# Inverse transform: left-over rows through DRAM scratch from tile 3 on, in four parts, with another scratch layout and two writes on ScalarE's queue

## The chip, the cores and the metric

The kernel runs on one core of a Trainium2 chip. The metric is the time of one execution in device microseconds (us). TensorE, VectorE, ScalarE and GpSimd compute; SyncE issues most of the DMAs, and ScalarE and GpSimd can issue some from their own queues.

## What is computed

An FNet-like block and a gated one, both with a residual, in float32. The weights of the first are a filter in the frequency domain:

```python
def _A_ref(x, w_r, w_i):
    B, S, D = x.shape                                  # 1, 2048, 640
    X = jnp.fft.rfft2(x, axes=(-2, -1))
    X = X * (w_r + 1j * w_i)
    return jnp.fft.irfft2(X, s=(S, D), axes=(-2, -1))

def _B_ref(x, w_gate, w_up, w_down):                   # 640 -> 1728 -> 640
    return ((x @ w_gate) * (x @ w_up)) @ w_down

h = x + _A_ref(_layernorm(x), w_r, w_i)
h2 = h + _B_ref(_layernorm(h), w_gate, w_up, w_down)
```

## The kernel before

The 2048 positions are 16 tiles of 128 rows (`NT`). The kernel has stages that follow each other on TensorE: the transform along 640 and 2048 forwards, the filter, the transform along 2048 backwards, the transform along 640 backwards (the inverse stage here), and the gated block in two halves of eight tiles.

The inverse stage takes tile after tile. For tile `t`, `id_mm(t)` (L731) multiplies four blocks of 128 frequencies from `qm` with the table `imt` (128x161 each); the trace shows two instructions for each. Of 642 frequency rows 130 are left over: 64 rows and one edge row for the real and for the imaginary part. They lie in `qr`, split in a high and a low half so that the fast type loses nothing, high in partitions 0 to 63, low in 64 to 127. There are two ways to multiply them:

- plain: five products of 128x322 straight from `qr`;
- stacked: four products of 162 columns with 99 rows each, for which high rows, low rows and high rows again stand below one another (`SI[t]`, three times 33). To be brought into that order the rows make a round trip: `ispread` writes them from `qr` to a DRAM scratch `ifar` (four DMAs and one for the edge rows), and `istack` reads them back (one DMA for 66 rows, one for 33).

Before the change tiles 0 to 4 are plain, tiles 5 to 15 are stacked. The scratch has two parts: tiles 5 to 8, and 9 to 15. `IPARTS` names three reads: tiles 5 to 8 and, once they are done, 12 to 15 go to a stretch of the tile `xt` (named `near` in the code, `xt` in the trace), tiles 9 to 11 go to the tile tagged `dC` (`si` in the trace).

After `id_mm`, `unfold` (L743) copies one half of the sum with ScalarE (`s`, L750), adds and subtracts on VectorE (`q`), folds out on VectorE or GpSimd (`yt`), and `is1_mm` multiplies the 128-point transform (`y<-yt,tab` in the trace). The order on TensorE is tile 0, 1, 2, 3, then `y` of tile 0, tile 4, `y` of tile 1, tile 5 and so on; `id_mm` runs three tiles ahead of `y`.

The last rows of `qr` are written on VectorE just before the stage: high rows at L562, low rows at L563, and row 0 of both halves for the edge at L559 and L560.

The order of the program is written out by hand (`manual_schedule`); each engine runs its own instructions in that order. SyncE's queue holds around the stage: the load of `raw` (`wlast`), part one of the scratch and its read, part two, two loads of `raw` (`wgu`, weights of the gated block), the read of tiles 9 to 11. The read of tiles 12 to 15 follows when tile 8's products have been issued (L742). Each DMA takes the next of eight landing semaphores and first waits that the DMA which used it before has landed.

Of the kernel before, what the change touches and what calls it, by code (L numbers as in the profile page):

```python
# [11 lines left out]
F32 = mybir.dt.float32  # L12
F32R = mybir.dt.float32r
# [3 lines left out]
P = 128  # L17
S, D, NF, FF = 2048, 640, 321, 1728
NT = S // P
# [6 lines left out]
RWHERE = ((1, 0), (0, 0), (1, 160), (0, 160))  # L26
RW = (160, 194, 162, 162)
PLAIN, MID = 5, 10
IPLAIN, IFAR = 5, 9
SUMS = 7  # L30
IPARTS = ((5, 4), (9, 3), (12, 4))
AGAIN = {0: (5, 3, "dC"), 1: (8, 2, "qt"), 4: (10, 3, 0), 7: (13, 3, 1)}
NR = 4
AHEAD = 5
# [15 lines left out]
def f32(ap):  # L50
    return ap.bitcast(F32)
# [29 lines left out]
def tile_spectral_glu(ctx: ExitStack, tc: tile.TileContext, x, wre, wim, wgu, wlast, wdown, wdlast,  # L81
                      cc, ci, fmain, frem, imain, irem, mm, out):
    nc = tc.nc
# [4 lines left out]
    far = ctx.enter_context(tc.tile_pool(name="far", bufs=1, space=bass.MemoryType.DRAM))  # L88
# [210 lines left out]
    def rest_high(a, b):  # L299
        act(s1r[:, 0, a:b], rest[:, a:b], AF.Copy)  # L300
# [114 lines left out]
    def load_mm(g, way):  # L415
        if g < NG:
            nc.sync.dma_start(mms[g % 4][:, way], mm[g][:, way])
# [165 lines left out]
    for g in range(NG - 1):  # L583
        s2_mm(g)
        load_mm(g + 4, 0)
        if g + 2 < NG:
            d_mm(g + 2)
        if g + 3 == NG:
            xt = home("big", [P, 2, 5, 2, 512], "xt", F32R)
            flat = xt[:, 1].rearrange("p k l n -> p (k l n)")  # L590
            irt, sirt = cut(flat, 0, 5, NQ), cut(flat, 5 * NQ, 4, 162)
            scrap, near = cut(flat, 2258, D), cut(flat, 2258 + D, 4, 4, P)
        if g == NG - 2:
            nc.gpsimd.dma_start(flat[:, 0:2258], irem)
        if g == NG - 2:
            s2_mm(g + 1)
            filt_half(g, 0, True, (lambda: is2_out(g - 2),))
        if g >= 1:
            is2_mm(g - 1)
            load_mm(g + 3, 1)  # L600
        if g < NG - 2:
            add = filt(g)
        else:
            direct, _ = filt_half(g, 1)
            direct()
            late = [filt_half(g + 1, 0), filt_half(g + 1, 1, True)]
            high, end, low, main, edges = is2_parts(g - 1)
            late[0][0]()
            high(copy)
            end(copy)  # L610
            low()
            late[0][1]()
            late[1][1]()
            main(slice(0, 4))
            edges(nc.gpsimd)
        if g + 3 < NG:
            load_w(g + 3)
        if g >= 4 and g in AGAIN:
            stack(*AGAIN[g])
        if g == 0:  # L620
            rest_high(MID, NG)
        elif g == 1:
            rest_low(MID, NG)
            qr = home("qr", [P, 2, NT, P], "qr", F32R)
        if g + 2 < NG:
            d_out(g + 2, (0,))
            if 1 <= g < NG - 3:
                high, end, low, main, edges = is2_parts(g - 1)
                high(copy)
                end(copy)  # L630
            d_out(g + 2, (1,))
            add()
            if 1 <= g < NG - 3:
                low()
                main(slice(0, 4))
                edges(nc.gpsimd)
        if g < 2:
            stack(*AGAIN[g])
        elif g == 2:
            spread(MID, NG)  # L640
        if g == 9:
            nc.sync.dma_start(cit, ci)
            nc.sync.dma_start(imt, imain)
# [62 lines left out]
    PE_, PY, YT, Z = {}, {}, {}, {}  # L706

    SI = {}
    ifar = [(a, far.tile([2, 2, 2, 33, b - a, P], F32, name="ifar")) for a, b in ((IPLAIN, IFAR), (IFAR, NT))]

    def ispread(a, o):
        ts = slice(a, a + o.shape[4])
        for h in (1, 0):
            for l in range(2):
                r = 64 * l + 31 * h
                nc.sync.dma_start(o[:, h, l, 1 - h:33].rearrange("b r t n -> r b t n"),
                                  f32(qr[r:r + 32 + h, :, ts]))
        e = f32(qr[0:65:64, 1, ts])
        nc.sync.dma_start(o[:, 0, :, 0].rearrange("b l t n -> l b (t n)"),
                          bass.AP(tensor=e.tensor, offset=e.offset,  # L720
                                  ap=[list(e.ap[0]), [0, 2], [1, P * o.shape[4]]]))

    def istack(t, n):
        o = near[:, :, 0:n] if t != 9 else home("dC", [P, 4, 3, P], "si", F32R)
        a, i = ifar[t >= IFAR]
        src = i[:, :, :, :, t - a:t - a + n].rearrange("b h l r t n -> (l r) (b h) (t n)")
        nc.sync.dma_start(f32(o[0:66]).rearrange("p q t n -> p q (t n)"), src)
        nc.sync.dma_start(f32(o[66:99]).rearrange("p q t n -> p q (t n)"), src[0:33])
        for i in range(n):
            SI[t + i] = o[:, :, i]  # L730

    def id_mm(t):
        ps = PE_[t] = pair("eo")
        main = [(b, o, 161, qm[:, c, t], imt[:, c]) for c, (b, o) in enumerate(((0, 0), (1, 0), (0, 161), (1, 161)))]
        if t not in SI:
            parts((ps[:, 0], ps[:, 1]), main,
                  [(b, qr[:, k, t], irt[:, c]) for c, b, k in ((0, 0, 0), (2, 0, 0), (1, 1, 1), (3, 0, 1), (4, 1, 1))])
            return
        parts((ps[:, 0], ps[:, 1]), main, [])
        for q, (b, h) in enumerate(((0, 0), (0, 1), (1, 0), (1, 1))):  # L740
            mmx(ps[:, b, 160 * h:160 * h + 162], SI[t][0:99, q], sirt[0:99, q], False, h == 1)
        if t == 8:  # L742
            istack(*IPARTS[2])  # L743

    def unfold(t, side, turns=(), extra=()):
        ps = PE_[t]
# [149 lines left out]
    for ts in (range(3), range(3, 6), range(6, 8)):  # L896
        n, t0 = len(ts), ts[-1] + 1
# [11 lines left out]
    tside[NT - 1] = []  # L909
    raw0 = home("dA", [P, 3, D], "raw0")  # L910
    jobs = load_direct(0, [raw0[:, i] for i in range(3)], mid=(
        lambda: ispread(*ifar[0]), lambda: istack(*IPARTS[0]), lambda: ispread(*ifar[1])))
    istack(*IPARTS[1])
    for i, (h, l) in enumerate((h, l) for hs, ls in jobs for h, l in zip(hs, ls)):
        aside[2 + i] += [h, l]
    id_mm(0)
# [287 lines left out]
    for n, (blk, p) in enumerate(steps):  # L1204
# [133 lines left out]
        else:  # L1338
            fs = down_products(*prev, (0, 1)) + down_products(*prev, (2, 3))
            flat = iter(sum(fs, []))  # L1340
# [221 lines left out]
```

## Time and profile before

| what | us |
|---|---|
| median of 3 runs (671.66 to 671.91) | 671.69 |
| the profiled execution | 671.72 |
| its span | 669.9 |
| TensorE busy in the span | 661.1 |
| VectorE, GpSimd, ScalarE busy | 469.1, 394.1, 321.6 |
| products of the inverse stage, first to last start | 106.8 to 148.3 |

Times inside the span count from its start. PE is TensorE's multiplication, PEld its weight load, which runs ahead of it; DVE is VectorE, ACT ScalarE, POOL GpSimd, SP SyncE, and SPq SyncE's queue of DMA issues. A name such as `eo<-xt,si` is the written tile and the read ones, and L121 is the line of the helper that issues nearly all products. The granted TensorE clock is 1.0 throughout. A row of an issue tells how long the queue was occupied by it, not how long the transfer took.

### The profile page before, as it was taken

Reading aid. Unit: us, or ns where it says so; the run is one execution under the profiler, and the core shown is the slowest. Engines: PE = TensorE matmul, PEld = TensorE weight load, DVE = VectorE, ACT = ScalarE, POOL = GpSimd, SP = SyncE. Lnnn points to the kernel's source line nnn. Section 1 sums busy time; section 2 is a strip of 40 time slices with the busy share of each in tenths; the row PEclk is TensorE's granted clock in tenths of the full one; section 3 lists DMA queues with packets and bytes.
Section 4 is the critical chain, followed back from the end, with each engine's and each line's share of the span. In section 5 each row is a group of like instructions: output and inputs, shape, how many; then the busy total and the mean of one; then the engine's idle time right before and its main releaser. Section 6 shows DMA issues by size and latency. Waiting matters only on the chain.

```text
span 669.9 us, 10244 instructions
## 1 busy us (share of the span) xinstructions
PE 661.1 (99%) x3695; PEld 588.4 (88%) x3695; DVE 469.1 (70%) x953; ACT 321.6 (48%) x621; POOL 394.1 (59%) x377
## 2 busy tenths in 40 slices
PE   7999999999999999999999999999999999999997
PEld 7999999887888888888888899888888888888887
DVE  6969997788767767594857567754757475757644
ACT  6977773585525244453626146534434251624220
POOL 3101124750397977968696445198786869697610
PEclk9999999999999999999999999999999999999999
DMA  8638874502212120142332467212011121212004
GB/s 316 230 111 279 245 250 144 172 2 79 79 40 80 39 79 21 33 105 60 98 79 83 95 132 261 79 40 73 14 37 75 41 78 40 79 40 80 1 0 158
DMA packets 48953, 66.12 MB, mean 99 GB/s; under 512 B 24082, under 2 KB 30670, under 8 KB 48774
## 3 DMA queue, kind: packets, MB, share of 16 engines
q1 hardware_dynamic: 48246, 62.91, 30.4%
q0 software_dynamic: 288, 2.16, 0.8%
q8 instruction: 29, 0.48, 0.3%
q10 hardware_dynamic: 368, 0.39, 0.2%
q14 instruction: 22, 0.18, 0.1%
HBM read 54.61 MB, written 10.84 MB: 98 GB/s over the span
## 4 chain that ended last, share of the span: by engine, by line
PE 95%; ACT 2%; DVE 2%; DMA 1%; issue 0%; DVEq 0%
PE e L121 50%; PE d L121 26%; PE eo L121 4%; PE y L121 2%; PE re L121 2%; PE u L476 2%; PE im L121 2%; PE im L527 2%; PE im L270 2%; PE ir L527 1%; DMA x<-in_x_dram 1%; ACT s L296 1%; ACT fold L212 0%; ACT fold L211 0%; PE y L803 0%
## 5 line engine op out<-in xcount | busy, mean ns | idle before, releaser
L121 PE MATMUL e<-xt,wst 128*128 128x512 f32 x864 | 211.1, 390 | 0.0
L121 PEld LDWEIGHTS e<-xt,wst 128*128 128x128 f32 x864 | 160.6, 188 | 31.7
L1082 DVE TENSOR_TENSOR x<-d,x 128x320 f32<-128x320 f32 x280 | 120.3, 482 | 41.2 <-PE d L121 37.0
L121 PE MATMUL d<-wd,ht 128*128 128x320 f32 x832 | 142.1, 309 | 0.0
L121 PEld LDWEIGHTS d<-wd,ht 128*128 128x128 f32 x832 | 129.6, 188 | 5.2
L996 POOL TENSOR_TENSOR wst<-raw,wst 128x1024 fp32r<-128x1024 f32 x23 | 55.5, 2412 | 69.4 <-ACT wst L995 69.4
L121 PE MATMUL e<-t,wst 128*128 128x512 f32 x360 | 94.0, 391 | 0.0
L121 PEld LDWEIGHTS e<-t,wst 128*128 128x128 f32 x360 | 66.7, 188 | 13.0
L121 PE MATMUL d<-wt,ht 128*128 128x320 f32 x360 | 68.9, 309 | 0.0
L1012 POOL TENSOR_TENSOR wst<-raw,wst 128x896 fp32r<-128x896 f32 (+1 forms) x46 | 65.3, 1445 | 0.2 <-ACT wst L1007 0.2
L121 PEld LDWEIGHTS d<-wt,ht 128*128 128x128 f32 x360 | 57.3, 188 | 0.8
L1098 ACT ACTIVATE ht<-e 128x512 fp32r<-128x512 f32 x44 | 26.4, 600 | 49.3 <-DVE e L1160 23.7
L1007 ACT ACTIVATE wst<-raw 128x896 fp32r<-128x896 f32 (+1 forms) x48 | 30.1, 676 | 31.2 <-POOL raw L1001 30.4
L1156 DVE TENSOR_TENSOR e<-e,h 128x512 f32<-128x512 f32 x24 | 16.8, 699 | 39.4 <-ACT wst L1007 23.2
L1057 DVE TENSOR_TENSOR x<-d,x 128x320 f32<-128x320 f32 x62 | 27.5, 485 | 22.5 <-PE d L121 22.4
L688 ACT ACTIVATE wd<-draw 128x320 fp32r<-128x320 f32 (+1 forms) x30 | 15.7, 561 | 55.2 <-POOL draw L698 52.4
L121 PE MATMUL e<-xt,wdir 128*128 128x512 f32 x180 | 41.9, 392 | 0.0
L1136 ACT ACTIVATE h<-e 128x512 f32<-128x512 f32 x24 | 14.3, 596 | 56.8 <-PE e L121 56.8
L121 PEld LDWEIGHTS e<-xt,wdir 128*128 128x128 f32 x180 | 33.4, 188 | 7.5 <-ACT xt L813 0.5
L1101 DVE TENSOR_TENSOR ht<-e,ht 128x512 fp32r<-128x512 f32 x54 | 36.9, 685 | 1.6 <-ACT ht L1098 1.3
L1153 ACT ACTIVATE h<-e 128x512 f32<-128x512 f32 x24 | 14.3, 597 | 46.6 <-PE e L121 46.6
L667 POOL TENSOR_TENSOR wd<-draw,wd 128x640 fp32r<-128x640 f32 x8 | 12.5, 1582 | 40.8 <-ACT wd L666 40.8
(241 smaller groups left out, 1190.6 us busy)
## 6 DMA issues: line engine op xcount, KB each, us to landing
raw<-in_wgu_dram SPq DMA_DIRECT2D x24, 640.0 KB
draw<-in_wdown_dram SPq DMA_DIRECT2D x24, 320.0 KB
wts<-in_wre_dram SPq DMA_DIRECT2D x16, 322.0 KB
x<-in_x_dram SPq DMA_DIRECT2D x15, 320.5 KB
out_dram<-x SPq DMA_DIRECT2D x15, 320.0 KB
bits<-in_mm_dram SPq DMA_DIRECT2D x32, 128.0 KB
wts<-in_wim_dram SPq DMA_DIRECT2D x9, 322.0 KB
zfar<-zr SPq DMA_DIRECT2D x32, 80.0 KB
```

The costliest lines, as they stand in the source:

```text
L121: nc.tensor.matmul(o, l, r, start=start, stop=stop, skip_group_check=True)
L527: nc.tensor.matmul(out, y[:, h, a:b], inv(g, h), start=n == 0, stop=n == len(ys) - 1)
L688: act(o[:, 0, a:a + n], src, AF.Copy)
L996: ptt(wa[:, 1], stage[:, 0:1024], f32(wa[:, 0]), op=OP.subtract)
L1007: act(ws[:, 0, o:o + b - a], stage[:, a:b], AF.Copy)
L1012: ptt(ws[:, 1, o:o + b - a], stage[:, a:b], f32(ws[:, 0, o:o + b - a]), op=OP.subtract)
L1057: tt(xv, ps[b][:, 0:320], xv, op=OP.add)
L1082: tt(xv, o, xv, op=OP.add)
L1098: act(hop[:, a, 0], src, AF.Copy)
L1101: engine.tensor_tensor(hop[:, a, 1], src, f32(hop[:, a, 0]), op=OP.subtract)
L1136: act(h0, oa, AF.Copy)
L1156: tt(ob, ob, h1, op=OP.add)
```

## The change

- Tiles 3 and 4 become stacked. `IPARTS` now lists four parts, tiles 3 and 4, 5 to 8, 9 to 11, 12 to 15, each with its tile: parts 0 and 2 the one tagged `dC`, parts 1 and 3 the stretch of `xt`.
- Each part has a scratch of its own. Its dims were (part of the spectrum, half, copy, row, tile, column), and are now (copy, row, part, half, tile, column), so that what one partition reads, four pieces of 512 bytes times the number of tiles, is one contiguous run. The stretch of `xt` is cut anew for each part, so that the run is contiguous there as well.
- The order is: write part 0, write part 1, read part 0, read part 1, the two `raw` loads, write part 2, read part 2, write part 3; the read of part 3 stays at tile 8.
- For part 0 the two writes with `h` = 1 go out on ScalarE's queue; all others stay on SyncE's.

```diff
-IPLAIN, IFAR = 5, 9
-IPARTS = ((5, 4), (9, 3), (12, 4))
+IPARTS = ((3, 2, "dC"), (5, 4, "near"), (9, 3, "dC"), (12, 4, "near"))
...
-            scrap, near = cut(flat, 2258, D), cut(flat, 2258 + D, 4, 4, P)
+            scrap, near = cut(flat, 2258, D), cut(flat, 2258 + D, 16 * P)
...
-    ifar = [(a, far.tile([2, 2, 2, 33, b - a, P], F32, name="ifar")) for a, b in ((IPLAIN, IFAR), (IFAR, NT))]
+    ifar = [far.tile([2, 33, 2, 2, n, P], F32, name="ifar") for _, n, _ in IPARTS]
-    def ispread(a, o):
-        ts = slice(a, a + o.shape[4])
+    def ispread(i, queue=nc.sync):
+        t, n, _ = IPARTS[i]
         for h in (1, 0):
             for l in range(2):
                 r = 64 * l + 31 * h
-                nc.sync.dma_start(o[:, h, l, 1 - h:33].rearrange("b r t n -> r b t n"),
-                                  f32(qr[r:r + 32 + h, :, ts]))
+                (queue if h else nc.sync).dma_start(ifar[i][l, 1 - h:33, :, h].rearrange("r b t n -> r b (t n)"),
+                                                    f32(qr[r:r + 32 + h, :, t:t + n]).rearrange("r b t n -> r b (t n)"))
...
-    def istack(t, n):
-        o = near[:, :, 0:n] if t != 9 else home("dC", [P, 4, 3, P], "si", F32R)
-        a, i = ifar[t >= IFAR]
-        src = i[:, :, :, :, t - a:t - a + n].rearrange("b h l r t n -> (l r) (b h) (t n)")
-        nc.sync.dma_start(f32(o[0:66]).rearrange("p q t n -> p q (t n)"), src)
-        nc.sync.dma_start(f32(o[66:99]).rearrange("p q t n -> p q (t n)"), src[0:33])
+    def istack(i):
+        t, n, tag = IPARTS[i]
+        if tag == "near":
+            o = cut(near, 0, 4, n, P)
+        else:
+            o = home(tag, [P, 4, n, P], "si", F32R)
+        src = ifar[i].rearrange("l r b h t n -> (l r) (b h t n)")
+        nc.sync.dma_start(f32(o[0:66]).rearrange("p q t n -> p (q t n)"), src)
+        nc.sync.dma_start(f32(o[66:99]).rearrange("p q t n -> p (q t n)"), src[0:33])
...
     jobs = load_direct(0, [raw0[:, i] for i in range(3)], mid=(
-        lambda: ispread(*ifar[0]), lambda: istack(*IPARTS[0]), lambda: ispread(*ifar[1])))
-    istack(*IPARTS[1])
+        lambda: ispread(0, nc.scalar), lambda: ispread(1), lambda: istack(0), lambda: istack(1)))
+    ispread(2)
+    istack(2)
+    ispread(3)
```

SyncE's queue from the load of `wlast` on, before the change (written and read tile, then partitions and elements):

```order
L665 DMA raw_1299<-in_wlast_dram 128x640
L716 DMA ifar<-qr 33x2x512 x2
L716 DMA ifar<-qr 32x2x512 x2
L719 DMA ifar<-qr 2x2x512
L727 DMA xt<-ifar 66x4x512
L728 DMA xt<-ifar 33x4x512
L716 DMA ifar<-qr 33x2x896 x2
L716 DMA ifar<-qr 32x2x896 x2
L719 DMA ifar<-qr 2x2x896
L665 DMA raw_1299<-in_wgu_dram 128x640 x2
L727 DMA si<-ifar 66x4x384
L728 DMA si<-ifar 33x4x384
```

The same place after it; L715 is the line of the writes, L718 of the edge rows, L728 and L729 of the reads:

```order
L664 DMA raw_1301<-in_wlast_dram 128x640
L715 DMA ifar<-qr 64x1x256 x2
L718 DMA ifar<-qr 2x2x256
L715 DMA ifar<-qr 66x1x512 x2
L715 DMA ifar<-qr 64x1x512 x2
L718 DMA ifar<-qr 2x2x512
L728 DMA si<-ifar 66x1024
L729 DMA si<-ifar 33x1024
L728 DMA xt<-ifar 66x2048
L729 DMA xt<-ifar 33x2048
L664 DMA raw_1301<-in_wgu_dram 128x640 x2
```

Eight writes stand ahead of the first read where five stood, and the first read is now that of tiles 3 and 4. The two writes missing from part 0 stand on ScalarE, between the last copy into `qm` and `s` of tile 0.

TensorE from tile 3's main products to those of tile 5, before:

```order
L121 MATMUL eo<-tab,qm 128x161 x4
L121 MATMUL eo<-xt,qr 128x322 x5
L121 MATMUL y<-yt,tab 128x320 x2
L121 MATMUL eo<-tab,qm 128x161 x4
L121 MATMUL eo<-xt,qr 128x322 x5
L121 MATMUL y<-yt,tab 128x320 x2
L121 MATMUL eo<-tab,qm 128x161 x4
```

And after:

```order
L120 MATMUL eo<-tab,qm 128x161 x4
L120 MATMUL eo<-xt,si 128x162 x4
L120 MATMUL y<-yt,tab 128x320 x2
L120 MATMUL eo<-tab,qm 128x161 x4
L120 MATMUL eo<-xt,si 128x162 x4
L120 MATMUL y<-yt,tab 128x320 x2
L120 MATMUL eo<-tab,qm 128x161 x4
```

Only the left-over products of tiles 3 and 4 differ, and they now read `si`, which comes by DMA. On VectorE and GpSimd no instruction moves.

More of the change, by code (lines that the diff above doesn't have):

```diff
@@ L715, in ispread @@
                 r = 64 * l + 31 * h
-                nc.sync.dma_start(o[:, h, l, 1 - h:33].rearrange("b r t n -> r b t n"),
-                                  f32(qr[r:r + 32 + h, :, ts]))
[L718 to L721, printed above, removed]
-    def istack(t, n):
-        o = near[:, :, 0:n] if t != 9 else home("dC", [P, 4, 3, P], "si", F32R)
-        a, i = ifar[t >= IFAR]
-        src = i[:, :, :, :, t - a:t - a + n].rearrange("b h l r t n -> (l r) (b h) (t n)")
[L727 to L730, printed above, removed]
+                (queue if h else nc.sync).dma_start(ifar[i][l, 1 - h:33, :, h].rearrange("r b t n -> r b (t n)"),
+                                                    f32(qr[r:r + 32 + h, :, t:t + n]).rearrange("r b t n -> r b (t n)"))
+        e = f32(qr[0:65:64, 1, t:t + n])
+        nc.sync.dma_start(ifar[i][:, 0, :, 0].rearrange("l b t n -> l b (t n)"),
+                          bass.AP(tensor=e.tensor, offset=e.offset, ap=[list(e.ap[0]), [0, 2], [1, P * n]]))
+    def istack(i):
[7 more added lines that the diff above has]
+        nc.sync.dma_start(f32(o[66:99]).rearrange("p q t n -> p (q t n)"), src[0:33])
+        for j in range(n):
+            SI[t + j] = o[:, :, j]
     def id_mm(t):
@@ L742, in id_mm @@
         if t == 8:
-            istack(*IPARTS[2])
+            istack(3)
     def unfold(t, side, turns=(), extra=()):
```

## The prediction

> **What bounds the kernel now.** I read the page first, then TensorE's waits, then the inverse stage engine by engine in order of time. The page says that TensorE is busy for nearly the whole span:
>
> ```profile
> span 669.9 us, 10244 instructions
> PE 661.1 (99%) x3695; PEld 588.4 (88%) x3695; DVE 469.1 (70%) x953; ACT 321.6 (48%) x621; POOL 394.1 (59%) x377
> ```
>
> TensorE's waits between 107 and 157 us, which is the inverse stage and what follows it, are one line (total, times, longest):
>
> ```profile
> PE eo L121 <- ACT qm L556: 0.3, 1, 0.3
> ```
>
> So what TensorE saves here shortens the span, and what it waits here lengthens it. TensorE in order of time (start, duration, line, output<-inputs), tiles 3, 4 and 5:
>
> ```profile
> 112.65 1.26 PE L121 MATMUL eo<-tab,qm 128*128 128x161 f32 x8
> 113.64 1.00 PE L121 MATMUL eo<-xt,qr 128*128 128x322 f32 x5
> 114.48 1.24 PE L121 MATMUL y<-yt,tab 128*128 128x320 f32 x4
> 115.56 1.26 PE L121 MATMUL eo<-tab,qm 128*128 128x161 f32 x8
> 116.55 1.01 PE L121 MATMUL eo<-xt,qr 128*128 128x322 f32 x5
> 117.40 1.24 PE L121 MATMUL y<-yt,tab 128*128 128x320 f32 x4
> 118.47 1.26 PE L121 MATMUL eo<-tab,qm 128*128 128x161 f32 x8
> 119.46 0.68 PE L121 MATMUL eo<-xt 99*128 99x162 f32 x4
> 119.98 1.28 PE L121 MATMUL y<-yt,tab 128*128 128x320 f32 x4
> ```
>
> A plain tile reads its left-over rows straight from `qr` (five products); a stacked one, tile 5, reads them from a tile that came through DRAM (four narrower products, input `xt`). The stacked tile is shorter, but its input must have landed. SyncE's queue for that round trip, each row one or more DMA issues:
>
> ```profile
> 107.04 2.19 SPq L716 DMA_DIRECT2D ifar<-qr  x4
> 109.28 0.57 SPq L719 DMA_DIRECT2D ifar<-qr  x1
> 111.28 0.29 SPq L727 DMA_DIRECT2D xt<-ifar  x1
> 111.63 0.39 SPq L728 DMA_DIRECT2D xt<-ifar  x1
> 112.06 2.10 SPq L716 DMA_DIRECT2D ifar<-qr  x4
> 114.20 0.51 SPq L719 DMA_DIRECT2D ifar<-qr  x1
> 114.75 3.62 SPq L665 DMA_DIRECT2D raw<-in_wgu_dram  x2
> 121.08 0.32 SPq L727 DMA_DIRECT2D si<-ifar  x1
> 121.44 0.39 SPq L728 DMA_DIRECT2D si<-ifar  x1
> ```
>
> The reader should see how tight it is: the first write goes out at 107.04, the read for tile 5 only at 111.28, and tile 5 wants it at 119.46. The change wants a read of the same kind for tile 3, whose left-over products start at 113.64.
>
> **The saving.** From the start of its main products to the start of `y`, tile 3 takes 114.48 - 112.65 = 1.83 us and tile 4 takes 117.40 - 115.56 = 1.84 us; the stacked tile 5 takes 119.98 - 118.47 = 1.51 us. Two tiles change their kind: 2 x 0.325 = 0.65 us, all on TensorE's path. Nothing else on TensorE, VectorE or GpSimd changes its place, so 0.65 us is the most that the change can give.
>
> **When the read for tile 3 is issued.** What the writes wait for are the last rows of `qr`, on VectorE, and on ScalarE the work around the two writes that now go out there:
>
> ```profile
> 107.78 0.21 DVE L559 CAST qr<-bits 1x128 fp32r<-1x128 f32 x1
> 108.03 0.28 DVE L560 TENSOR_TENSOR qr<-bits,qr 1x128 fp32r<-1x128 f32 x1
> 106.34 0.66 ACT L556 ACTIVATE qm<-im 128x256 f32<-128x256 f32 x2 [1.00 <-PE im L527]
> 109.17 0.44 ACT L750 ACTIVATE s<-eo 128x322 f32<-128x322 f32 x1 [2.17 <-PE eo L121]
> ```
>
> ScalarE is free from 107.00 to 109.17. Its two issues cost nothing if they end before 109.17: the first can go at 107.05, the second needs the low rows. What is queued behind them is `s` of tile 0, which would lose whatever they overrun. Their price on SyncE is in these rows:
>
> ```profile
> L716 SPq DMA_DIRECT2D ifar<-qr x8: 311/397/594, 107.0 to 113.7; - x8
> 108.18 1.04 SPq L716 DMA_DIRECT2D ifar<-qr  x2
> ```
>
> Two issues at the longest 0.594 us, with the second begun at 107.77 or so, end by 108.4. That cover is large enough, so I cost them at nothing. They take two issues off SyncE, but SyncE's own first write now holds row 0, which VectorE finishes at 107.99, so SyncE begins at 108.05 and not at 107.04. Before the read it must issue three writes of part 0 and all five of part 1, since the program puts part 1 ahead of the first read. Three such issues took 108.18 to 109.85, that is 1.67 us; five took 112.06 to 114.71, that is 2.65 us. So 108.05 + 1.67 + 0.05 + 2.65 + 0.05 = 112.5 us for the read's first issue. With every issue at the shortest of the rows (6 x 0.311, 2 x 0.51, 8 gaps of 0.05) it would be 111.3; with all at the longest (6 x 0.594, 2 x 0.57, the same gaps) 113.2. I take 112.5, whole batches as measured. The read's own wait, for part 0's writes, should be over: the last part 0 write goes out by 109.7, and in the old order SyncE went on 2.0 us after that same issue (109.28 to 111.28).
>
> **How long the read takes.** Nearest is the read of tiles 9 to 11 (`si`), which ran with nothing beside it. Its sizes, then the stretches around it (busy time by engine, granted clock, DMA share, GB/s), and at the head the end of a write:
>
> ```profile
> si<-ifar SPq DMA_DIRECT2D x1, 396.0 KB
> si<-ifar SPq DMA_DIRECT2D x1, 198.0 KB
> 110.50:111.00 0.50, 0.50 (x6) 0.50 (x5) 0.47 (x2) 0.00 (x0) 0.38 (x1) 1.00 0.03 12
> 114.50:121.50 7.00, 7.00 (x41) 6.05 (x41) 4.77 (x12) 1.95 (x4) 3.08 (x4) 1.00 0.91 288
> 121.50:122.00 0.50, 0.50 (x6) 0.50 (x5) 0.50 (x1) 0.25 (x1) 0.50 (x1) 1.00 0.08 31
> 122.00:123.00 1.00, 1.00 (x9) 0.92 (x8) 0.96 (x5) 0.63 (x2) 0.97 (x1) 1.00 0.56 99
> 123.00:125.50 2.50, 2.50 (x17) 2.22 (x16) 2.50 (x6) 1.63 (x4) 2.48 (x2) 1.00 0.69 203
> ```
>
> Issued at 121.08, it moves little until 122.0 (0.92 us), 99 GB/s in its first microsecond, then 203 GB/s. From the last bytes of a write (just after 110.5) to SyncE going on (111.28) is some 0.5 to 0.7 us; I put 0.5 us behind a read too. The new read is 2 tiles of 66 and 33 rows, 264 + 132 = 396 KB. Slow start kept: 0.92 + 1.0 + 297/203 + 0.5 = 3.9 us. At 203 GB/s throughout: 0.92 + 1.95 + 0.5 = 3.4 us. At the 288 GB/s that the busy stretch shows: 0.92 + 1.4 + 0.5 = 2.8 us. I take 3.4: the pieces grow from 1.5 KB (384 elements) to 4 KB (1024), which should help against the `si` row, but nothing shows a lone read of this size without the slow start.
>
> A rule to weigh against that row: the Trainium skill, DMA: Bandwidth & Descriptors, section "Anatomy of one DMA — SWDGE (gpsimd) path", fits a DMA's time as about 2.0 us plus its bytes at 436 GB/s. For 396 KB that would be an estimate of 2.9 us, and the sum below would come to 672.8 in place of 673.3. The trace measures longer: the second `raw` load waits for the first read of tiles 5 to 8 (528 KB), and its rows are
>
> ```profile
> SPq L665 <- DMA xt<-ifar: 0.2, 1, 0.2
> 116.72 1.65 SPq L665 DMA_DIRECT2D raw<-in_wgu_dram  x1
> ```
>
> so that read, issued at 111.28, was over only just before 116.72, 5.4 us later. By the fit of the Trainium skill it would be an estimated 3.2 us, so the measured row decides and I keep 3.4.
>
> **The sum.** Landing: 112.5 + 3.4 = 115.9 us. Tile 3 wants it at 113.64, so TensorE waits 2.25 us. Behind the waiting product are `y` of tile 0 and all of tile 4, and ScalarE and VectorE wait for tile 3 itself; on SyncE the reads of tiles 5 to 8 and the raw loads stand behind the read. Net: 2.25 - 0.65 = +1.6 us, on the profiled execution's 671.72 us (span 669.9 and 1.82 around it): 673.3 us. That execution is 0.03 us above the median of 671.69, which I ignore. The ends: issue 111.3 and 2.8 us give a landing at 114.1, a wait of 0.5 and a net of -0.15; issue 113.2 and 3.9 us give 117.1, 3.5 and +2.8.
>
> The rest costs nothing. Tile 4's rows come in the same read. The `raw` loads stay where they were on SyncE (before 114.75; now behind two more issues at about 114.5), and ScalarE's wait for them hides 1.07 us already and moves later with TensorE:
>
> ```profile
> 121.75 0.74 ACT L666 ACTIVATE wdir<-raw 128x640 fp32r<-128x640 f32 x1 [1.07 <-DMA raw<-in_wgu_dram]
> ```
>
> The writes of parts 2 and 3, behind the raw loads now, have until tiles 9 and 12, over 8 us later. Bigger pieces for those reads shorten transfers nobody waits for.
>
> **The rivals.** *The read is quicker than the `si` row* (ends on the other side: not slower by what can be measured). If packets of 4 KB run at 288 GB/s and the issues at their median 0.397 us (6 x 0.397 + 2 x 0.54 + 0.4 = 3.86, so issue at 111.9), landing is 114.7, the wait 1.1, the net +0.45: 672.2 us. For it: the pieces really are larger, and ScalarE's part runs beside SyncE's. Against: 0.69 is the share of the DMA engines that these reads reached, and the slow first microsecond stands in each read of scratch. It decides at a landing of 115.6: earlier, and the loss is under 1.34 us, which is 0.2% of 671.69 and about what a measurement of this kernel can tell from no change. The 2.9 us worked out from the Trainium skill fall on this side.
>
> *No wait at all.* The stacked rows land by 113.64 and 0.65 us is won: 671.1 us. It needs the read issued by 110.8 even at 2.8 us; only a SyncE that issues faster than any row would do that.
>
> *The second read is what comes late.* Tiles 5 to 8 come behind part 1's writes: the last goes out at 111.95, SyncE goes on 2.0 us later at 113.9, and if the first takes 5.4 us again and the second is over its 264 KB at 203 GB/s later, 1.3 us, they land at 120.6. Tile 5 would want them at 119.46 - 0.65 + 2.25 = 121.1. The spare is 0.5 us; if they take 1.0 us more than that, to 121.6, the net is 121.6 - 118.8 = +2.8: 674.5 us. Against: larger pieces.
>
> *TensorE's clock drops in the wait.* The granted clock is 1.00 also in this early stretch with TensorE busy 0.45 of 2.00 us, which holds its longest wait:
>
> ```profile
> 10.00:12.00 2.00, 0.45 (x4) 0.32 (x3) 1.90 (x11) 2.00 (x7) 0.77 (x2) 1.00 1.04 395
> ```
>
> ```profile
> PE im L270 <- DVE bits L287: 2.2, 2, 1.5
> ```
>
> If a wait of 3.5 us (the long end) did halve it for as long again, that would add some 1.7 us to +2.8: 676.2 us. The Trainium skill, TensorE: Matmul & The Clock Gate, section "What's actually happening", says that the clock halves after at least one idle window of about 3.4 us; TensorE's longest wait in the trace is 1.5 us, so no run here shows it.
>
> **How the numbers follow.** Forecast (net +1.34 to +2.6) 0.50. Quicker read (0 to +1.34) 0.34. No wait (-0.65 to 0) 0.06. Second read late 0.05, clock 0.02. For a gain beyond 1.34 us I see no mechanism, and leave 0.03 for what I have not seen. So slower 0.57, same 0.40, faster 0.03. The range 671.6 to 674.4 leaves out the gains and the best of the quicker reads below, and the two late rivals and the longest issues above, under 2 in 10. The forecast alone would be 673.05 to 674.4.
>
> **What would show it.** In the profile after: a wait of TensorE's weight load for a DMA `si<-ifar` of 1.9 to 3.2 us just after 113.6, tiles 3 and 4 at four products of 162 columns (0.68 us), the first `si` issue near 112.5, no wait at tile 5, the clock at 1.00. I am wrong if `si` is issued before 111.5, if the landing comes by 115.2, or if TensorE waits at another place.

## The result, and the profile after

The changed kernel takes 678.01 us (median of 5 runs, 676.82 to 678.59), the kernel before beside it 671.69 us (5 runs, 671.66 to 672.36). The ratio is 1.0089, with a 95% interval of 1.0078 to 1.0101: slower, 6.3 us in place of the 1.6 us forecast and above the range's 674.4. The profiled execution took 678.01 us. The page's first lines after the change:

```profile
span 676.2 us, 10257 instructions
PE 663.7 (98%) x3693; PEld 590.0 (87%) x3693; DVE 468.9 (69%) x953; ACT 321.4 (48%) x621; POOL 394.3 (58%) x377
```

TensorE issues two products fewer and is yet busy 2.6 us longer than before (663.7 against 661.1): some of its work became slower. And TensorE's waits in the stretch from 100 to 165 us (total, times, longest) hold a row that was not there:

```profile
PE eo L120 <- DMA si<-ifar: 4.1, 1, 4.1
```

TensorE in order of time (start, duration, line, output<-inputs, in brackets the idle time ahead and who ended it), from tile 3's main products to those of tile 5:

```profile
112.57 1.26 PE L120 MATMUL eo<-tab,qm 128*128 128x161 f32 x8
117.98 1.11 PE L120 MATMUL eo<-xt,si 99*128 99x162 f32 x4 [4.15 <-DMA si<-ifar]
118.89 2.41 PE L120 MATMUL y<-yt,tab 128*128 128x320 f32 x4
121.10 2.27 PE L120 MATMUL eo<-tab,qm 128*128 128x161 f32 x8
123.05 0.73 PE L120 MATMUL eo<-xt,si 99*128 99x162 f32 x4
123.62 1.27 PE L120 MATMUL y<-yt,tab 128*128 128x320 f32 x4
124.73 1.26 PE L120 MATMUL eo<-tab,qm 128*128 128x161 f32 x8
```

Two things are to be seen: one wait for the read of tiles 3 and 4, and behind it products that take about twice their time (`y` 2.41 us where it took 1.24, the main products 2.27 where they took 1.26), until tile 4's left-over products are normal again (0.73). Why they are slow stands in the stretches of the same time (length, busy time of PE, PEld, DVE, ACT and POOL, then the granted clock, DMA share, GB/s):

```profile
113.90:116.00 2.10, 0.00 (x0) 0.00 (x0) 0.79 (x2) 0.00 (x0) 1.06 (x1) 1.00 0.53 142
116.00:118.00 2.00, 0.02 (x1) 0.05 (x1) 0.00 (x0) 0.00 (x0) 0.00 (x0) 0.58 0.66 216
118.00:123.00 5.00, 5.00 (x16) 4.21 (x17) 1.64 (x4) 0.44 (x1) 0.00 (x0) 0.50 0.85 239
123.00:124.00 1.00, 1.00 (x8) 0.92 (x8) 0.50 (x1) 0.13 (x1) 0.94 (x1) 0.92 0.73 273
```

The granted clock fell to 0.50 in the middle of the wait and stayed there until shortly after 123. The trace's record of the clock has half speed from 116.33 to 123.16 us, 6.83 us in all.

The books close at tile 5. Its main products start at 124.73 where they started at 118.47, 6.26 us later, and the whole span is 6.3 us longer, so nothing behind tile 5 matters. Of the 6.26: tile 3's main products start 0.08 us earlier (112.57 for 112.65); the left-over products could follow 0.99 us behind them, at 113.56, and start at 117.98, +4.42; from there to tile 5's main products it takes 6.75 us, where before it took 118.47 - 113.64 = 4.83, which the two shorter tiles would make 4.18, so +2.57 from the half clock; and -0.65 from the shorter tiles. That is -0.08 + 4.42 + 2.57 - 0.65 = 6.26. The sum takes the 0.65 us over from the forecast and finds the 2.57 as what is left beside it, so it is no check of either; e4 below has the same products at full clock and takes 4.22 us for this way, which makes the saving 0.61 and the half clock 2.53 us.

Why tile 3's rows came so late is seen on SyncE's queue (start, time that the queue was held, number of issues):

```profile
107.72 1.33 SPq L715 DMA_DIRECT2D ifar<-qr  x2
109.09 0.72 SPq L718 DMA_DIRECT2D ifar<-qr  x1
109.86 3.03 SPq L715 DMA_DIRECT2D ifar<-qr  x4
112.94 0.57 SPq L718 DMA_DIRECT2D ifar<-qr  x1
113.62 0.35 SPq L728 DMA_DIRECT2D si<-ifar  x1
```

Four writes of part 1 hold the queue 3.03 us; before, the same four writes of tiles 5 to 8 took 2.19 us (at 107.04). The read is issued at 113.62, not at 112.5, and by the trace its two DMAs landed at 117.66 and 117.85, 4.2 us after that. ScalarE's queue shows the same for its two writes:

```profile
106.71 2.33 ACTq L715 DMA_DIRECT2D ifar<-qr  x2
109.15 0.44 ACT L751 ACTIVATE s<-eo 128x322 f32<-128x322 f32 x1 [2.49 <-PE eo L120]
```

They hold ScalarE until 109.04. Tile 0's products were through at 107.53 + 1.26 = 108.79 us, and `s` would have started at about 108.83, as before (0.04 us behind 107.87 + 1.26): it is 0.3 us late. Tile 0's main products start 0.34 us earlier than before in this execution (106.44 for 106.78), tile 3's only 0.08, so the lateness may have cost TensorE up to 0.26 us. (In e4 and e6 below, where `s` is not late, tile 3's main products stand 5.87 us behind tile 0's, as before; here it is 6.13.)

### The profile page after: what moved, and what is told of

Read it like the earlier page. It is cut to its first block, busy times and chain, and to the rows that moved or that the text cites. A ratio compares the mean times of both kernels' runs of the same rounds, so it can differ in the third digit from the quotient of the medians.

```text
span 676.2 us, 10257 instructions
## 1 busy us (share of the span) xinstructions
PE 663.7 (98%) x3693; PEld 590.0 (87%) x3693; DVE 468.9 (69%) x953; ACT 321.4 (48%) x621; POOL 394.3 (58%) x377
## 4 chain that ended last, share of the span: by engine, by line
PE 93%; ACT 2%; DVE 2%; DMA 1%; SPq 1%; issue 0%; DVEq 0%
PE e L120 50%; PE d L120 26%; PE eo L120 3%; PE y L120 3%; PE re L120 2%; PE u L475 2%; PE im L120 2%; PE im L526 2%; PE im L269 2%; PE ir L526 1%; DMA x<-in_x_dram 1%; SPq L715 1%; DMA si<-ifar 1%; ACT s L295 1%; ACT fold L211 0%; ACT fold L210 0%
```

## Experiments

The theory after this profile: the loss is the wait for the read of tiles 3 and 4 and the half clock that the wait sets off, and the wait is longer than forecast because the new layout makes each write hold its queue longer. In the new layout the row dim and the dim of the spectrum's part merge into one (66 or 64 rows of one piece in the order's listing, `64x1x256`, where it had `33x2` and `32x2`). The rivals: the layout or ScalarE's writes cost time by themselves; it is the order of the reads; the slow read is a matter of how many DMA engines it uses; the slow products come from something other than the clock. All figures in us; "before" is the kernel before, run beside each.

| kernel | median (range, runs) | before | ratio (95% interval) |
|---|---|---|---|
| e1_plain34 | 671.96 (671.57 to 672.56, 10) | 671.81 | 1.0002 (0.9993 to 1.0012) |
| e2_read_first | 680.26 (678.49 to 680.56, 4) | 671.81 | 1.0117 (1.0102 to 1.0133) |
| e3_keep_busy | 677.07 (675.73 to 677.82, 4) | 671.81 | 1.0073 (1.0058 to 1.0088) |
| e4_unmerged | 675.27 (673.78 to 675.55, 4) | 671.81 | 1.0050 (1.0033 to 1.0067) |
| e5_old_layout | 675.35 (675.21 to 675.63, 4) | 671.94 | 1.0053 (1.0036 to 1.0070) |
| e6_all_sync | 679.00 (677.88 to 679.86, 4) | 671.94 | 1.0105 (1.0090 to 1.0120) |
| e7_sixteen | 676.29 (674.32 to 677.28, 4) | 671.94 | 1.0062 (1.0044 to 1.0080) |
| e8_unmerged_busy | 673.75 (673.41 to 673.99, 9) | 671.94 | 1.0027 (1.0017 to 1.0037) |
| e9_from_four | 673.52 (672.60 to 675.52, 11) | 671.89 | 1.0029 (1.0020 to 1.0038) |
| e10_plain34_unmerged | 671.89 (671.41 to 672.61, 11) | 671.89 | 1.0002 (0.9993 to 1.0011) |
| e11_write_early | 672.28 (671.72 to 673.10, 11) | 672.10 | 1.0005 (0.9996 to 1.0014) |

**e1_plain34: the change without its first part.** Tiles 3 and 4 stay plain; layout, contiguous reads and ScalarE's writes stay in.

```diff
-IPARTS = ((3, 2, "dC"), (5, 4, "near"), (9, 3, "dC"), (12, 4, "near"))
+IPARTS = ((5, 4, "near"), (9, 3, "dC"), (12, 4, "near"))
...
-        lambda: ispread(0, nc.scalar), lambda: ispread(1), lambda: istack(0), lambda: istack(1)))
-    ispread(2)
-    istack(2)
-    ispread(3)
+        lambda: ispread(0, nc.scalar), lambda: istack(0)))
+    ispread(1)
+    istack(1)
+    ispread(2)
```

> Tiles 3 and 4 plain again, so part 0 of the scratch is gone; the new layout, the order and the two writes on ScalarE stay for the first part that is left (tiles 5 to 8). Theory (the loss is the wait for the rows of tile 3 and what that wait does to TensorE's clock): no wait of TensorE for a DMA, clock 1.00, 671.4 to 672.2 us, the time of the kernel before. Rival (the layout or the writes on ScalarE cost by themselves): over 673 us with tiles 3 and 4 plain.

It runs as the kernel before, and TensorE waits for no DMA. So neither the layout nor ScalarE's writes cost anything that can be measured while nobody waits for the read, and the rival that they cost time by themselves falls. It is close, though: the read of tiles 5 to 8 is issued at 111.93, its second DMA lands at 119.43, and tile 5's stacked products start at 119.56. With the unmerged layout of e4 below in the same place, e10_plain34_unmerged, the ratio is again 1.0002:

> Tiles 3 and 4 plain, three parts, unmerged writes, contiguous reads: the layout alone with its dear writes mended. Theory (contiguous pieces neither shorten a read nor cost anything): no wait for a DMA, 671.5 to 672.2 us, the read of tiles 5 to 8 issued at about 111.2 and landed within 6.3 to 7.6 us as with the pieces of before. Rival (the contiguous pieces help where nothing else is in the way): the read lands in under 5.5 us.

Its read was issued at 111.30 and landed at 118.89, again without a wait. The contiguous reads by themselves win nothing either.

**e4_unmerged: the whole change with the scratch in another order.** The part comes behind the half, so that rows and parts no longer merge and a write keeps the form `33x2`; what a partition reads is still one contiguous run.

```diff
-ifar[i][l, 1 - h:33, :, h].rearrange("r b t n -> r b (t n)")
+ifar[i][l, 1 - h:33, h].rearrange("r b t n -> r b (t n)")
...
-        src = ifar[i].rearrange("l r b h t n -> (l r) (b h t n)")
+        src = ifar[i].rearrange("l r h b t n -> (l r) (h b t n)")
...
-SI[t][0:99, q], sirt[0:99, q]
+SI[t][0:99, 2 * h + b], sirt[0:99, q]
```

> The scratch has its half ahead of its part (copy, row, half, part, tile, column), so that what a partition reads is still one run, but a write is 33 rows of 2 pieces again and not 66 rows of one. Theory (the writes in the form of 66 rows of one piece take SyncE 0.83 to 0.89 us each against 0.31 to 0.58 before, which delays the read): issues back at 0.3 to 0.6 us, the read of part 0 issued at 112.0 to 112.7 instead of 113.6, the wait at tile 3 about 3 us, less or no halved clock, 673.5 to 675.5 us. Rival (the form does not matter, the issue times come from the queue): 677 to 678.6 us.

SyncE's queue in its profile:

```profile
107.99 0.80 SPq L715 DMA_DIRECT2D ifar<-qr  x2
108.84 0.57 SPq L718 DMA_DIRECT2D ifar<-qr  x1
109.47 1.68 SPq L715 DMA_DIRECT2D ifar<-qr  x4
111.20 0.49 SPq L718 DMA_DIRECT2D ifar<-qr  x1
111.81 0.35 SPq L728 DMA_DIRECT2D si<-ifar  x1
```

The same bytes from the same place: 0.80 us for two writes in place of 1.33, 1.68 for four in place of 3.03. The read goes out 1.8 us earlier, and TensorE waits

```profile
115.77 0.65 PE L120 MATMUL eo<-xt,si 99*128 99x162 f32 x4 [1.92 <-DMA si<-ifar]
```

1.92 us, less than the 3 us or so that were expected. The median falls by 678.01 - 675.27 = 2.7 us. The merged form is thus shown to be the cause of the late issue. The four runs fall into two kinds: the profiled one took 673.78 with a mean clock of 0.999, the other three 675.10 to 675.55 with 0.997.

**e5_old_layout: the same four parts in the layout of before.** Four pieces of 1 KB for each partition, `33x2` writes, nothing contiguous.

```diff
-    ifar = [far.tile([2, 33, 2, 2, n, P], F32, name="ifar") for _, n, _ in IPARTS]
+    ifar = [far.tile([2, 2, 2, 33, n, P], F32, name="ifar") for _, n, _ in IPARTS]
...
-        src = ifar[i].rearrange("l r b h t n -> (l r) (b h t n)")
+        src = ifar[i].rearrange("b h l r t n -> (l r) (b h) (t n)")
...
```

> Four parts, tiles 3 and 4 stacked, the order and the two writes on ScalarE as in the change, but each part's scratch keeps the layout of before (part, half, copy, row, tile, column): a partition reads four pieces, a write is 33 or 32 rows of 2 pieces. Theory (the contiguous pieces do nothing for the read, and only cost through the form of the writes): the read of part 0 issued at 111.5 to 112.3, landed within 3.6 to 4.2 us as in the other runs, wait at tile 3 of 1.7 to 2.7 us, 673.5 to 676 us. Rival (the contiguous pieces shorten the read): the read takes 4.8 us or more, wait over 3 us, 676 us or more.

The read was issued at 111.81, as in e4, and landed 4.17 us later (e4: 3.82). The medians, each beside its own before, are 3.4 and 3.5 us above it: in these two executions contiguous pieces of 4 KB in place of 1 KB shorten the read by a third of a microsecond, and the medians differ by nothing that can be told. The profile of e5 holds the clearest picture of the clock. First TensorE, then the stretches:

```profile
116.12 0.65 PE L120 MATMUL eo<-xt,si 99*128 99x162 f32 x4 [2.31 <-DMA si<-ifar]
116.60 1.46 PE L120 MATMUL y<-yt,tab 128*128 128x320 f32 x4
117.86 2.35 PE L120 MATMUL eo<-tab,qm 128*128 128x161 f32 x8
119.81 1.18 PE L120 MATMUL eo<-xt,si 99*128 99x162 f32 x4
```

```profile
113.80:116.10 2.30, 0.01 (x1) 0.01 (x1) 0.87 (x2) 0.00 (x0) 1.06 (x1) 1.00 0.71 212
116.10:117.50 1.40, 1.38 (x8) 1.16 (x9) 0.00 (x0) 0.44 (x1) 0.00 (x0) 1.00 0.95 255
117.50:121.00 3.50, 3.50 (x15) 3.31 (x14) 2.13 (x5) 0.00 (x0) 1.06 (x1) 0.51 0.88 239
121.00:123.00 2.00, 2.00 (x13) 1.68 (x12) 0.80 (x3) 1.06 (x2) 0.00 (x0) 1.00 0.59 211
```

The wait was 2.3 us and over; TensorE had been busy for 1.4 us at full clock when the clock fell, from 117.57 to 120.98, 3.41 us. So the drop can come after a wait that is shorter than the stretch itself, and behind it rather than in it. One of the four runs took 675.21 us with a clock of 1.0; it was not profiled, and what it lost instead stays open.

The records of the clock show more. Full speed lasted 109.23 us up to the drop in the changed kernel, 119.47 in e2, 112.64 in e5 and in e6: 32, 35, 33 and 33 times 3.413 us. The clock thus changes only at points that are 3.413 us apart, wherever the wait begins, and one can add up TensorE's work between two such points. The last such stretch before the drop in e5; the one of e7 (below) that holds most of its wait; and the last whole stretch of the kernel before, with what follows it:

```profile
114.16:117.57 3.41, 1.45 (x8) 1.25 (x9) 0.51 (x2) 0.44 (x1) 1.06 (x1) 1.00 0.82 227
112.31:115.72 3.41, 1.59 (x12) 1.34 (x10) 1.92 (x5) 0.44 (x1) 2.12 (x2) 1.00 0.80 180
665.55:668.96 3.41, 0.91 (x7) 0.64 (x5) 0.98 (x2) 0.00 (x0) 0.00 (x0) 1.00 0.52 192
668.96:669.94 0.98, 0.00 (x0) 0.00 (x0) 0.00 (x0) 0.00 (x0) 0.00 (x0) 0.50 0.00 0
```

TensorE was busy 1.45 of 3.41 us in e5, idle 1.96, and the clock fell. In e7 it waited longer, 2.52 us, but the wait lies across such a point, 1.82 us ahead of it and 0.69 behind, and the clock stayed; so it did in the profiled execution of e4, whose 1.92 us are split into 0.73 and 1.19. In all thirteen traces the clock fell behind every stretch at full clock with 1.96 us or more of idle time and behind none with 1.82 or less. Half speed lasted one stretch where that stretch held no idle time (e5), and two where the first held some (1.65 us in the changed kernel, 0.55 in e2, 0.27 in e6). Whether a wait between some 2 and 3.6 us (twice 1.82, an estimate) costs the clock is thus a matter of where it falls between these points. No experiment moved a wait on purpose to test this, and the executions that were not profiled may be of this kind or not.

**e3_keep_busy and e8_unmerged_busy: the same wait, filled with work.** To tell the half clock from the wait, TensorE repeats tile 3's main products while the read is under way: four times in the changed kernel, three times in e4's. Nothing is left out; each repeat starts the sum anew.

```diff
-        parts((ps[:, 0], ps[:, 1]), main, [])
+        for _ in range(3 if t == 3 else 1):
+            parts((ps[:, 0], ps[:, 1]), main, [])
```

> Tile 3's main products are run four times (the first start of each clears the sum, so the last run alone counts): 3.0 us of work that nobody needs, put into the wait. Theory (some 2.5 us of the loss are the halved clock after a long idle stretch): TensorE idles only 1.0 to 1.5 us, the clock stays at 1.00 and the time falls to 675.0 to 676.0 us though more work is done. Rival (the clock has nothing to do with the idle stretch, or costs little): 678 us, or more by the extra work.

> The kernel with the unmerged writes, and tile 3's main products run three times (2.0 us that nobody needs, in the wait; the last run alone counts). Theory (its scatter from 673.8 to 675.6 us is the clock, halved in some executions after an idle stretch of only 1.9 us): no execution shows a lower clock, all lie in 673.2 to 674.3 us. Rival (the scatter is the DMA's): times from 673.8 to 675.6 as without the extra products.

e8 in order of time, and its clock:

```profile
112.93 3.46 PE L120 MATMUL eo<-tab,qm 128*128 128x161 f32 x24
116.14 0.67 PE L120 MATMUL eo<-xt,si 99*128 99x162 f32 x4
118.75 0.68 PE L120 MATMUL eo<-xt,si 99*128 99x162 f32 x4
```

```profile
112.00:115.00 3.00, 3.00 (x24) 3.00 (x23) 2.44 (x6) 0.44 (x1) 1.43 (x3) 1.00 0.67 205
115.00:118.00 3.00, 3.00 (x21) 2.69 (x20) 0.13 (x2) 0.44 (x1) 0.69 (x1) 1.00 0.88 221
118.00:123.00 5.00, 5.00 (x32) 4.37 (x31) 4.22 (x10) 1.93 (x4) 1.76 (x2) 1.00 0.73 237
```

TensorE does two rounds of products more (2 x 0.99 = 2.0 us), and the kernel is 1.5 us faster than e4 (673.75 against 675.27); all nine runs show a clock of 0.999 or 1.0, where three of e4's four had 0.997. That the half clock follows from the idle time is thus shown. What is left, 673.75 - 671.94 = +1.8 us, is nearly all the wait: the read lands at 116.00, tile 3's left-over products would have followed at 113.92 and start at 116.14, 2.2 us, less the 0.65 saved. This comes near the +1.6 that the prediction had worked out, but in part by luck: against tile 3's main products the read is issued some 0.6 us earlier than forecast and takes 3.9 us in place of 3.4, and the two errors nearly cancel.

In the layout of the change (e3) the clock stays up as well (0.999 or 1.0 in all four runs, where the changed kernel had 0.994 to 0.997), but the edit wins less, 677.07 against 678.01, with intervals of the two ratios that touch, and misses what was expected by 1 us. Two waits of TensorE for a DMA are left:

```profile
PE eo L120 <- DMA xt<-ifar: 0.8, 1, 0.8
PE eo L120 <- DMA si<-ifar: 0.5, 1, 0.5
```

Tile 5 now waits for the second read, which landed at 124.18. In the changed kernel it landed at 123.44 and tile 5's stacked products start at 125.73, so the half clock had hidden this read. So the rival of the second read was real, but stood behind the other. A third wait in e3's profile, 0.9 us at 170.6 in the gated block, is for VectorE (`ht`); the changed kernel's profile does not have it, and its cause is not shown.

**e2_read_first: the first read ahead of part 1's writes.**

```diff
-lambda: ispread(1), lambda: istack(0), lambda: istack(1)))
+lambda: istack(0), lambda: ispread(1), lambda: istack(1)))
```

> The read of part 0 is issued ahead of the writes of part 1. Theory: the read goes out at about 111 us, as soon as part 0 has landed, and lands at about 115; TensorE waits 1.0 to 1.7 us at tile 3, too short for the clock to drop. Part 1 is then written 2 to 3 us later and its read lands at 122 to 123, so a second wait of 1.5 to 3 us appears at tile 5: 673.5 to 676 us in all. Rival (the wait at tile 3 is the read's own 4.2 us, not the writes ahead of it): wait at tile 3 still over 3 us, 677 us or more.

```profile
PE eo L120 <- DMA xt<-ifar: 4.4, 1, 4.4
PE eo L120 <- DMA si<-ifar: 1.2, 1, 1.2
```

The first read goes out at 111.14 and lands at 115.02, 3.9 us later with nothing read beside it. Tile 3 waits 1.2 us, but the second read is issued at 117.60 and lands at 124.94, and tile 5 waits 4.4 us; the clock is at half from 124.53 to 131.35, 6.83 us again. The time, 680.26, is above what was expected: the wait was moved, and grew (1.5 to 3 us were expected at tile 5). The order that the change chose was the better of the two.

**e6_all_sync: no writes on ScalarE.** `ispread(0)` in place of `ispread(0, nc.scalar)`.

> The change with all writes on SyncE's queue. Theory (each write in the form of 66 rows holds its queue for 0.8 to 1.4 us, so two more on SyncE delay the read): read of part 0 issued at 114.3 to 115.0 instead of 113.6, wait at tile 3 longer by 0.7 to 1.4 us, s of tile 0 no longer late (0.2 us back), the clock halved for the same two windows or more: 678.5 to 681 us. Rival (ScalarE's queue and SyncE's share what makes the issues slow, so it gains nothing): read issued within 0.3 us of 113.6, 677.5 to 678.5 us.

The read is issued at 114.58, 0.96 us later than in the changed kernel, and TensorE's wait is 4.9 us in place of 4.1. The median is 1.0 us higher, though the intervals of the two ratios (1.0090 to 1.0120, and 1.0078 to 1.0101) touch. So in these two profiles ScalarE's queue takes 0.7 to 1.0 us off the path, and the 0.3 us by which `s` came late is small beside that.

**e7_sixteen: reads cut so that they use all DMA engines.** In the trace a read of 66 or 33 rows runs on 11 of the 16 engines. Here, in e4's layout, each is cut into 64, 32, 2 and 1 rows.

```diff
-        nc.sync.dma_start(f32(o[0:66]).rearrange("p q t n -> p (q t n)"), src)
-        nc.sync.dma_start(f32(o[66:99]).rearrange("p q t n -> p (q t n)"), src[0:33])
+        for a, b, r in ((0, 64, 0), (66, 98, 0), (64, 66, 64), (98, 99, 32)):
+            nc.sync.dma_start(f32(o[a:b]).rearrange("p q t n -> p (q t n)"), src[r:r + b - a])
```

> The kernel with the unmerged writes, each read cut into rows 0 to 63, rows 66 to 97 and two small ones (2 rows, 1 row), so that most bytes come in DMAs of 64 and 32 rows. Theory (reads of 66 and 33 rows use 11 of the 16 DMA engines, which is the 0.69 share in the trace): the lone read of part 3 (792 KB) reaches a share near 1.0 and lands in 4.5 to 5.5 us instead of 6.5 to 6.9; the read of part 0, with two more issues, gains 0.3 us at most: 673.3 to 675.8 us in all. Rival (the rate of these reads is set by something else): part 3's read stays at 6 us or more and a share of 0.7.

Not faster: 676.29, and TensorE waits longer than the 1.92 us of e4:

```profile
116.42 0.65 PE L120 MATMUL eo<-xt,si 99*128 99x162 f32 x4 [2.52 <-DMA si<-ifar]
```

(This profiled execution kept its clock and took 674.32 us; the other three, at 0.995 to 0.997, took 675.76 to 677.28.) The read of tiles 12 to 15, which has the queue to itself, took from 131.78 to 138.43, 6.65 us, where e4's took 131.06 to 137.95, 6.9 us. The engines did move the bytes faster, at mean DMA shares of 1.16 and 1.07 in the two fullest microseconds by the profile's count, where e4 had 0.75 and 0.78; but the four issues of a read held the queue 1.71 us where e4's two took 0.69, and its bytes began only at 133.0, 1.3 us behind the first issue where e4's began 0.9 behind. So the cut wins nothing as a whole; what the number of engines alone would be worth is not shown.

**e9_from_four and e11_write_early: a version meant to win.** If a read cannot be there for tile 3, the stacked tiles can begin at tile 4, and the first parts can be made small. Both are in e4's layout.

```diff
-IPARTS = ((3, 2, "dC"), (5, 4, "near"), (9, 3, "dC"), (12, 4, "near"))
+IPARTS = ((4, 1, "dC"), (5, 2, 0), (7, 2, 8 * P), (9, 3, "dC"), (12, 4, 0))
...
     ispread(2)
     istack(2)
     ispread(3)
+    istack(3)
+    ispread(4)
```

> Stacked from tile 4 on, in five parts (4; 5 and 6; 7 and 8; 9 to 11; 12 to 15), unmerged writes. Theory (a read lands some 3.5 to 4 us after its issue, and what matters is that this is before the tile wants it): tile 4's read is issued at 111.3 to 112.2 and lands at 114.8 to 116.2, ahead of the 116.5 us at which tile 4 wants it; the reads of 5 and 6 and of 7 and 8 land ahead too. No wait for a DMA, clock 1.00, one tile's 0.33 us won: 671.3 to 671.9 us, below what the comparison can tell. Rival (the small reads get into one another's way): a wait at tile 4 or 5 of over 0.5 us, 672.3 us or more.

Tiles 4 to 8 come without a wait, as expected, but tile 9 waits:

```profile
116.59 0.68 PE L120 MATMUL eo<-xt,si 99*128 99x162 f32 x4
131.24 0.65 PE L120 MATMUL eo<-xt,si 99*128 99x162 f32 x4 [1.26 <-DMA si<-ifar]
```

SyncE held the read of tiles 7 and 8 until 120.17, for the writes that it needs, and the writes of tiles 9 to 11 stood behind it; their read went out at 125.56 and landed at 131.11. (Two of the eleven runs, at 675.4 and 675.5, show a clock of 0.997.) In e11 those writes go out ahead of it:

```diff
     ispread(2)
-    istack(2)
     ispread(3)
+    istack(2)
     istack(3)
```

> As e9_from_four (scratch in the order that is not merged, parts of tiles 4; 5 and 6; 7 and 8; 9 to 11; 12 to 15), with the writes of tiles 9 to 11 put ahead of the read of tiles 7 and 8 on SyncE's queue. Nothing is left out. Theory (in e9 the read of tiles 9 to 11 was late only because its writes stood behind a read that waited until 120.2 us, so that it was issued at 125.56 and landed at 131.1, 1.3 us late): the read of tiles 9 to 11 goes out by 122 to 123 us and lands by 128 to 129, TensorE waits for no DMA, its clock stays at 1.00 in every run, and the time is 671.3 to 671.9 us, the 0.33 us of one tile won, which is too little to be told from no change. Rival (the round trips share a bandwidth, and a read moved forward makes another late): a wait of 0.5 us or more appears at tile 7 or still at tile 9, and the time is 672.3 us or more.

TensorE's waits in the stretch from 100 to 165 us are then these two, neither of them for a DMA:

```profile
PE ir L526 <- DVE y L500: 0.3, 1, 0.3
PE eo L120 <- ACT qm L555: 0.3, 1, 0.3
```

The read of tiles 9 to 11 is issued at 121.40 and lands at 127.34, and the profiled execution takes 671.72 us. The 0.33 us of one tile cannot be told from no change (1.0005, 0.9996 to 1.0014); the median, 672.28, is above the 671.3 to 671.9 that were expected, as is that of the kernel before beside it. So a version with more stacked tiles runs without a loss that could be measured; one that measurably beats the kernel before was not found.

## Why the prediction was wrong

- **The saving, 0.65 us.** Nearly right: 0.61. In e4 it is 4.22 us from tile 3's left-over products to tile 5's main ones (115.77 to 119.99), before 4.83, and no product shows a lower clock.
- **When the read is issued, 112.5.** Wrong: 113.62. The step costed each write by rows of before, "whole batches as measured", 1.67 + 2.65 us. Those rows are of the form `33x2` and `32x2`, and the order's listing showed `66x1` and `64x1` for the new ones. In that form two writes took 1.33 and four 3.03 us of the queue: with the edge rows 2.09 us for three issues and 3.65 for five, 1.4 us more than the two terms, of which 0.3 was won back because the first write went out at 107.72 and not at 108.05. e4 has the old form back, and issues at 111.81, 0.7 us ahead of the forecast: with the right form the step was even cautious.
- **ScalarE's two writes at nothing.** Wrong by a little. They took 2.33 us, not the 1.2 at most that the step allowed, and `s` of tile 0 came 0.3 us late; the named cover, free until 109.17, was all used. What it cost TensorE is 0.26 us at most, and in e1, with nobody waiting for the read, nothing that can be measured.
- **How long the read takes, 3.4 us.** Wrong: 4.2 us in the changed kernel, 3.9 alone in e2, 3.8 in e4, 4.2 in e5. The end "slow start kept", 3.9 us, was the right one; the gain from larger pieces, for which the step itself had no row, is a third of a microsecond where it could be compared (e4 and e5). The fit from the Trainium skill, DMA: Bandwidth & Descriptors, section "Anatomy of one DMA — SWDGE (gpsimd) path", an estimated 2.9 us, lies some 0.9 us or more under every one of these; that section is on GpSimd's path, and these reads went out from SyncE.
- **The sum, a wait of 2.25 us.** 4.42 us: 1.1 us from the issue, 0.8 from the read, 0.1 between landing and product, 0.1 since tile 3 was there earlier, on top of 2.25.
- **The clock at 0.02.** This is the step that failed most: some 2.5 us of the 6.26. The prediction took the row of 10 to 12 us, TensorE 0.45 of 2.00 us busy at clock 1.00, as evidence against, and asked for a wait of 3.5 us. But that row shows only that a wait of 1.5 us can pass; it has no wait of the length that was forecast, 2.25. Nor is it so that no trace at hand showed a drop: the clock of the kernel before is not at 1.0 throughout, but falls at 668.96, behind a stretch of 3.41 us in which TensorE was busy for 0.91 and idle for no more than 2.50 us, at the end of its work. e5 shows the drop after 2.31 us; e4, whose profiled execution waited 1.92 us and kept its clock, had a lower one in the other three. The Trainium skill, TensorE: Matmul & The Clock Gate, section "What's actually happening", has a free-running window of about 3.4 us, and the traces agree with that length: half speed in the inverse stage lasted 3.41 us or twice that in each record. Its condition, at least one idle window, differs from the runs: in the changed kernel the clock fell at 116.33, when TensorE had been idle for 2.5 us and busy for 0.9 of the 3.41 us before. By the traces here the idle time that is enough lies between 1.82 us (e7, kept) and 1.96 us (e5, fell).
- **The rivals.** "No wait" and "quicker read" did not happen. "Second read late" was there behind the first, as e2 and e3 show, and cost nothing in the changed kernel.

So two steps failed: the wait was 4.42 us in place of 2.25, above all because the writes were costed by rows of another form, and the clock, put at 0.02, fell and cost another 2.5 us. The range missed for one reason: the two late ends, the issue and the read, and the clock were priced as separate accidents. The wait they add up to is what sets off the clock, so they come together.

## What to carry to other kernels

Before a product that follows close behind a DMA is made to depend on it, price the wait twice: its length, and half a clock stretch behind it (here 1.7 us for each 3.41 us) as soon as it is in the order of 2 us (up to some 3.6 us, by the estimate above, it is a matter of chance whether the clock falls, and executions can differ); work that fills the wait costs less than the idle time. When a layout is changed so that reads are contiguous, look at the form that the writes take on their queue: a dim that merges there made each issue hold the queue 1.5 to 3 times as long. A read whose length hardly changed with its pieces, and was not helped by being cut for more engines, is best moved earlier, by the order of the writes ahead of it, and each reordering is to be followed to the next read in the queue.

## What the runs showed of the hardware

- In the first two parts of the changed kernel a write from 66 merged rows held the queue 0.82 to 1.42 us and one from 64 merged rows 0.57 to 0.65 us, where 33 and 32 rows of two pieces held it 0.29 to 0.55 us in e4's first two parts, on SyncE and on ScalarE alike, for the same bytes.
- The lone read of tiles 12 to 15 (792 KB) took 6.8 us in pieces of 2 KB (before), 6.5 us (after) and 6.9 us (e4) in contiguous 8 KB, 6.65 us cut for 16 engines (e7). That of 594 KB took 5.2 us in pieces of 1.5 KB (before) and 5.1 us in contiguous 6 KB (after), that of 396 KB 3.9 us (e2): it is the bytes that tell, far more than the pieces.
- The clock's half-speed stretches were 3.41 us (e5) or 6.83 us (after, e2, e6), also when the work had begun again before the stretch began (e5, 1.4 us at full clock). In e4 the mean clock was lower in three executions and not in the fourth. It changed only at points 3.413 us apart, and fell where TensorE had been idle for 1.96 us or more between two of them (1.82 us did not do it).
